# DeltaNet and max-out layer in one kernel: the order of the opening, and the first chunk's links by halves of the heads

## The chip, the cores and the metric

The kernel runs on one NeuronCore of a Trainium2 chip. A NeuronCore has a matrix engine (TensorE, in the profile PE, its weight loads PEld), a vector engine (VectorE, DVE), a scalar engine (ScalarE, ACT), a general engine (GpSimd, POOL) and a synchronising engine (SyncE, SP). Each runs its own list of instructions in order; DMA transfers are issued by SP, ACT or POOL. The metric is the device time of one execution in microseconds (us), as a median over executions.

## The reference

For 4 batches and 8 heads, 768 tokens with head size 48, the first half is a delta rule; its output, tokens by 384, goes through a layer of three products whose maximum is taken, and an output product:

```
k_n = k / (norm(k) + 1e-06)
for t in range(S):
    y[:, :, t] = einsum('bhd,bhde->bhe', q[:, :, t], state)
    v_old = einsum('bhde,bhd->bhe', state, k_n[:, :, t])
    state += beta_t * einsum('bhd,bhe->bhde', k_n[:, :, t], v_t - v_old)
x = y.transpose(0, 2, 1, 3).reshape(B * S, H * D)
out = max(x @ w1, x @ w2, x @ w3) @ w_out
```

The queries read the state before the step's own update. The four weights come in a 64-bit format (384 x 768 and 768 x 384).

## The kernel before

**Tiles.** The 768 tokens are cut into 12 chunks of 64. A unit n is two batches of one chunk (24 units); chunk c holds units 2c and 2c+1, and its 128 partitions are 64 tokens by 2 batches. Four units, that is two chunks, make a group m. Within a chunk the recurrence is solved as a triangular system: `turn` (L327) transposes keys and queries on PE and copies them to `kqt`, `gram` (L391) multiplies keys with keys (`at`) and keys with queries (`pt`, multiplied by a triangular mask at L412). `at` is written to DRAM and read back by `blocks` (L450) as 32 x 32 blocks, one block to a partition; `solve` (L470) takes the norms from the diagonal (L245 on ACT, then DVE) and runs a substitution on DVE, pairs of L508 and L512. For the first two groups it solves blocks of 16 (`FINE`), 15 pairs. The solved blocks go to DRAM (L517) and come back as `ut` (L526).

**Links.** For each of the first four chunks a chain of links follows, every one a set of small matmuls and an eviction from PSUM: `halves_z` (p_e, L574; it also transposes `ut` to `t` on DVE, L579), `halves_u` (p_f, L595; evictions with a minus sign at L603 and L605; then `turn_t1`, L558), `join_z` (p_z, L616), `join_u` (p_j, L629; evictions L631, L632), `old_k` and `old_q` (products with the state, none for chunk 0), `new` (p_u, L675), `step` (the state, p_s, L698), `to_y` (p_y, L715) and `to_x` (p_x, L732), whose copy `xt` is what the feed-forward part reads. `copied` (L777) splits an eviction of chunk 0 between ACT and DVE.

**Weights.** A weight is 24 pieces. `fetch` (L188) loads one into `w_bits` (5 buffers); `weights` (L198) converts it: an Abs (L211) and a product (L220) on ACT, a clamp (L215) on POOL, and for the piece before it two steps on DVE (L230, L234) and a sum on POOL (L238). Every step of the generator does the first half for one piece and the second half for the piece before.

**Order.** From the start to `by_hand.close()` (L936) every engine's list is in the order of the program text. Then, in the first feed-forward group (L993 to L1023), only PE's list is written by hand: `ffn(0)` gives 31 steps, the first 18 of 256 tokens each (matmuls p_h, L797; a maximum on DVE, L807), and after each step one conversion, one fetch, and the links that `FIRST` and `EARLY_LINKS` name for that step are written; three steps of the second group's solve belong to each of the first seven. There the framework's planner orders the lists of the other engines. The first nine steps read the tokens of chunk 0, the next nine those of chunk 1. Later groups are again all by hand.

**Opening.** Key loads of units 0 to 5 are issued on SP and ACT, half each (L151); units 6 and 7 later on ACT alone (L875). `busy` (L850) issues matmuls whose result nobody reads: six at the start, three after the first solve (L896), and one of 256 columns after each of six links (`between`, L905). The first squares and norms (L868, L876) scale the values of chunks 0 and 1 (L277).

## Time and profile before

| | |
|---|---|
| median of 4 executions | 601.01 us (599.02 to 601.82) |
| the profiled execution, its own time | 599.02 us |
| its span in the profile | 597.2 us |
| busy PE, DVE, ACT, POOL | 551.2, 350.5, 141.0, 120.3 us |
| first matmul of the feed-forward part (p_h) | 69.14 us |
| the tenth group of p_h, the first for chunk 1 | 113.91 us |
| PE busy from 150 to 300 us | 150.00 us |
| PE busy from 0 to 70 us | 45.40 us |
| DVE busy from 70 to 150 us | 69.23 us |

The profile gives for each instruction its engine, its line in the kernel, what it writes and reads, its start and length, and what its engine waited for before it. A row of the timeline reads: start, length, engine, line, operation, written tile <- read tile, shapes, count, and in brackets the idle time before it with what ended it. ACTq and SPq are the DMA issues of ACT and SP. A row of the table of windows gives the busy time of each engine in a stretch of the span, then the clock that TensorE was granted as a share of full, the DMA's share and its rate.

### The profile page before, as it was taken

Reading aid. Unit: us, or ns where it says so; the run is one execution under the profiler, and the core shown is the slowest. Engines: PE = TensorE matmul, PEld = TensorE weight load, DVE = VectorE, ACT = ScalarE, POOL = GpSimd, SP = SyncE. Lnnn points to the kernel's source line nnn. Section 1 sums busy time; section 2 is a strip of 40 time slices with the busy share of each in tenths; the row PEclk is TensorE's granted clock in tenths of the full one; section 3 lists DMA queues with packets and bytes.
Section 4 is the critical chain, followed back from the end, with each engine's and each line's share of the span. In section 5 each row is a group of like instructions: output and inputs, shape, how many; then the busy total and the mean of one; then the engine's idle time right before and its main releaser. Section 6 shows DMA issues by size and latency. Waiting matters only on the chain.

```text
span 597.2 us, 18730 instructions
## 1 busy us (share of the span) xinstructions
PE 551.2 (92%) x8120; PEld 324.6 (54%) x8120; DVE 350.5 (59%) x792; ACT 141.0 (24%) x281; POOL 120.3 (20%) x209
## 2 busy tenths in 40 slices
PE   6358969868999999999999999999999999999997
PEld 5235757756655555545555555545555455554444
DVE  2466699769359675499873699763898522211110
ACT  3224455644311122121112111221211111010000
POOL 6014544491010062000633002800001000000000
PEclk9555766998999999999999999999999999999999
DMA  8999874862430272454565283743743202210002
GB/s 132 161 231 179 190 165 126 206 126 54 90 46 8 75 161 62 85 116 113 143 143 120 64 133 93 187 113 57 121 93 80 46 1 56 60 47 0 0 0 54
DMA packets 159506, 58.78 MB, mean 98 GB/s; under 512 B 141184, under 2 KB 153280, under 8 KB 159424
## 3 DMA queue, kind: packets, MB, share of 16 engines
q1 hardware_dynamic: 141664, 43.52, 36.4%
q10 hardware_dynamic: 14560, 9.24, 6.2%
q0 software_dynamic: 3200, 4.82, 3.3%
q8 instruction: 64, 1.05, 0.8%
q14 instruction: 18, 0.15, 0.1%
HBM read 40.21 MB, written 17.30 MB: 96 GB/s over the span
## 4 chain that ended last, share of the span: by engine, by line
PE 63%; DVE 5%; DMA 4%; SPq 4%; issue 1%; ACT 0%; POOL 0%; DVEq 0%; ACTq 0%; POOLq 0%
PE p_h L797 39%; PE p_o L821 13%; PE p_g L402 2%; PE p_u L675 2%; PE p_y L715 2%; PE p_s L698 1%; DMA kpad<-in_k_dram 1%; PE p_k L647 1%; PE p_q L647 1%; SPq L366 1%; PE p_j L629 1%; DMA y_x<-y 1%; SPq L115 1%; PE p_z L616 1%; DVE y_bl L512 1%
## 5 line engine op out<-in xcount | busy, mean ns | idle before, releaser
L797 PE MATMUL p_h<-xt,w_sb 128*128 128x512 f32 (+1 forms) x702 | 303.1, 577 | 1.2 <-DVE xt L783 1.2
L797 PEld LDWEIGHTS p_h<-xt,w_sb 128*128 128x128 f32 x702 | 130.1, 194 | 122.5 <-issue 112.1
L807 DVE TENSOR_TENSOR h<-h,p_h 128x512 f32<-128x512 f32 (+1 forms) x78 | 50.2, 643 | 105.2 <-PE p_h L797 105.0
L821 PE MATMUL p_o<-wo_sb,h 128*128 128x384 f32 x288 | 94.6, 487 | 0.0
L821 PEld LDWEIGHTS p_o<-wo_sb,h 128*128 128x128 f32 x288 | 54.2, 190 | 37.2 <-issue 1.0
L512 DVE TENSOR_TENSOR y_bl<-y_bl,tmp 128x31 f32<-128x31 f32 (+20 forms) x139 | 53.6, 386 | 4.7
L277 POOL TENSOR_TENSOR v_t<-v_t,nrm 128x768 f32<-128x768 f32 x12 | 18.0, 1497 | 189.5 <-DMA turned<-in_k_dram 83.1
L366 POOL DMA_DIRECT2D turned<-in_q_dram x96 | 52.3, 552 | 3.6 <-POOL turned L361 3.1
L508 DVE TENSOR_TENSOR tmp<-x_bl,y_bl 128x31 f32<-128x31 f32 (+20 forms) x139 | 45.9, 330 | 4.0
L805 ACT COPY h<-p_h 128x512 f32<-128x512 f32 (+1 forms) x39 | 21.5, 552 | 109.9 <-PE p_h L797 109.8
L402 PE MATMUL p_g<-kqt 48*64 48x64 f32 (+1 forms) x1280 | 33.2, 252 | 8.9 <-ACT kqt L342 6.5
L402 PEld LDWEIGHTS p_g<-kqt 48*64 48x64 f32 x1280 | 28.0, 151 | 17.5 <-ACT kqt L342 8.5
L829 ACT COPY o_sb<-p_o 128x384 f32<-128x384 f32 x24 | 11.4, 476 | 82.0 <-PE p_o L821 78.6
L215 POOL TENSOR_SCALAR mant<-mant 128x384 f32<-128x384 f32 x24 | 13.6, 568 | 50.3 <-ACT mant L211 50.2
L558 DVE STREAM_TRANSPOSE t<-ut 32x256 f32<-32x256 f32 x48 | 20.8, 433 | 4.8 <-DMA ut<-y_d 4.0
L238 POOL TENSOR_TENSOR w_sb<-mant,up 128x384 int32<-128x384 int32 x18 | 18.1, 1005 | 18.9 <-DVE mant L234 15.7
L420 ACT COPY at<-p_g 128x512 f32<-128x512 f32 x20 | 11.6, 584 | 42.0 <-DVE pt L412 39.5
L230 DVE TENSOR_SCALAR mant<-mant 128x384 uint32<-128x384 uint32 x24 | 13.8, 577 | 11.1 <-POOL mant L215 11.0
L412 DVE TENSOR_TENSOR pt<-p_g,mask 128x512 f32<-128x512 f32 x24 | 16.4, 686 | 6.5 <-PE p_g L402 6.3
L632 DVE TENSOR_SCALAR ut<-p_j 32x512 f32<-32x512 f32 x12 | 8.3, 689 | 20.2 <-ACT ut L631 20.1
L667 ACT COPY qs<-p_q 128x768 f32<-128x768 f32 x11 | 8.8, 798 | 46.4 <-DVE v_t L659 27.6
L675 PEld LDWEIGHTS p_u<-v_t,ut 64*64 64x64 f32 x768 | 13.6, 142 | 9.5 <-issue 6.7
(111 smaller groups left out, 514.7 us busy)
## 6 DMA issues: line engine op xcount, KB each, us to landing
at_d<-at SPq DMA_DIRECT2D x42, 128.0 KB
v_t<-in_v_dram SPq DMA_DIRECT2D x24, 192.0 KB
w_bits<-in_moe_w_dram ACTq DMA_DIRECT2D x12, 384.0 KB
turned<-in_q_dram POOLq DMA_DIRECT2D x96, 48.0 KB, 3.0
turned<-in_k_dram SPq DMA_DIRECT2D x96, 48.0 KB
out_dram<-o_sb SPq DMA_DIRECT2D x48, 96.0 KB
kpad<-in_k_dram SPq DMA_DIRECT2D x38, 96.0 KB
y_x<-y SPq DMA_DIRECT2D x16, 192.0 KB
```

The source lines that it names most:

```text
L238: nc.gpsimd.tensor_tensor(out=dst.bitcast(I32), in0=mant_v.bitcast(I32), in1=up_v, op=ALU.add)
L277: nc.gpsimd.tensor_tensor(out=vts[c], in0=vts[c], in1=nrm[:, :, :, None].to_broadcast([128, 2, H, D]), op=ALU.mult,)
L366: (nc.sync, nc.gpsimd)[i].dma_start(out=t[p0 : p0 + 32, bb, at : at + NP * 2 * D].rearrange("p (j x) -> p j x", j=NP), in_=(k, q)[i][2 * b ...
L402: nc.tensor.matmul(p_g[rows(bb ^ (g * i)), par, c0 : c0 + C * (1 + whole)], kq[:, 0], kq if whole else kq[:, i],)
L508: nc.vector.tensor_tensor(out=t_v, in0=row.to_broadcast(t_v.shape), in1=column.to_broadcast(t_v.shape), op=ALU.mult,)
L512: nc.vector.tensor_tensor(out=rest, in0=rest, in1=t_v, op=ALU.subtract)
L558: nc.vector.transpose(out=t1[c % NU][block(bb ^ g), g], in_=ut[c % NU][block(bb), g, :, 0:BL])
L675: nc.tensor.matmul(p_v[rows(bb ^ g), g, h], ut[c % NU][rows(bb), g, h], rhs[rows(bb), g, h],)
L797: nc.tensor.matmul(p_h, w_sb[i][:, t, f * 128 : (f + 1) * 128], xt[:, t, lo : lo + w], start=(t == 0), stop=(t == KT - 1),)
L805: nc.scalar.copy(h, p_h)
L807: nc.vector.tensor_tensor(out=h, in0=h, in1=p_h, op=ALU.max)
L821: nc.tensor.matmul(p_o, hs[f][:, i * 128 : (i + 1) * 128], wo_sb[:, f], start=(f == 0), stop=(f == FT - 1),)
```

## The change

The opening is written in another order, and the links take the heads of chunk 0 in two halves.

- Only units 0 to 3 are loaded on both queues; 4 and 5 follow on SP, 6 and 7 on SP after the first value load. The copy of unit 1's turned keys goes to DVE and that of its gram to ACT; its stores are split between SP and ACT.
- The first squares stand behind `blocks(0)`; `ksq` shares the buffers of `o_sb` instead of those of the conversions.
- The query grams of units 0 and 1 are evicted by a copy on ACT ahead of the substitution and masked in place on POOL, and `scale(0)` and the first conversion stand there too; so do the key grams of units 6 and 7, whose stores (`to_dram`) come after the solved blocks.
- Three fetches and two conversions follow the reads of `ut`; then one conversion behind each link (none between p_f and p_z), all fetches on SP. The opening begins nine conversions and finishes eight; before, eight and seven.
- `heads_of` gives for chunk 0 two halves of the heads, each in a PSUM tile of its own, evicted by ACT and DVE in turn, and for other chunks one whole set, evicted by ACT. `halves_t`, ahead of p_e, transposes `t` in three instructions instead of two, so that the second tile's rows are exchanged there and z is copied without an exchange. `halves_u` has two evictions on each engine for a set instead of four, `turn_t1` three transposes instead of four.
- The six `between` matmuls go, and of the three after the solve two remain.
- `halves_z(1)` is done in the opening, and `FIRST` names the later links of chunk 1 up to two steps earlier. The squares and norms of chunks 2 and 3 are written at steps 8 and 9 instead of both at 8.

The diff, cut:

```diff
-    for n in range(6):
+    for n in range(4):
         load_k(n, both_queues)
...
-            ksq = work.tile([128, H, D], FP32, name="ksq", tag="up", bufs=2)
+            ksq = work.tile([128, H, D], FP32, name="ksq", tag="o_sb")
...
-    def first_norms(ksum, kflip):
+    def flipped(kflip):
...
+        return p_n
+
+    def first_norms(ksum, p_n):
...
-        nc.scalar.copy(
+        copy(
...
+    def masked(t, of, engine=nc.vector):
+        engine.tensor_tensor(
+            out=by_par(t), in0=of,
+            in1=mask[:, None, None, :].to_broadcast([128, 2, NP, C]), op=ALU.mult,
+        )
+
-    def gram(n, parts=(0, 1), queues=one_queue, copy=nc.scalar.copy):
+    def gram(n, parts=(0, 1), queues=one_queue, copy=nc.scalar.copy, later=False):
...
-            nc.vector.tensor_tensor(
-                out=by_par(pt), in0=p_v[:, :, :, 1],
-                in1=mask[:, None, None, :].to_broadcast([128, 2, NP, C]),
-                op=ALU.mult,
-            )
+            if later:
+                copy(by_par(pt), p_v[:, :, :, 1])
+            else:
+                masked(pt, p_v[:, :, :, 1])
...
+        if queues:
+            to_dram(n, queues)
+
+    def to_dram(n, queues=one_queue):
+        m, cc, g, at = n // 4, n % 4 // 2, n % 2, ats[n]
...
     def turn_t1(c):
 
-        for bb, g in TILES:
+        t, u_t = t1[c % NU], ut[c % NU]
+        nc.vector.transpose(out=t[:, 0], in_=u_t[:, 0, :, 0:BL])
+        for bb in range(2):
             nc.vector.transpose(
-                out=t1[c % NU][block(bb ^ g), g], in_=ut[c % NU][block(bb), g, :, 0:BL]
+                out=t[block(1 - bb), 1], in_=u_t[block(bb), 1, :, 0:BL]
             )
 
     fine = {}
 
+    def halves_t(c):
+
+        fine[c] = [square("t") for g in range(2)]
+        src = [ut[c % NU][:, g].rearrange("p h x -> p (h x)") for g in range(2)]
+        dst = [t.rearrange("p h x -> p (h x)") for t in fine[c]]
+        nc.vector.transpose(out=dst[0], in_=src[0])
+        for bb in range(2):
+            nc.vector.transpose(out=dst[1][rows(1 - bb)], in_=src[1][rows(bb)])
+
+    def heads_of(c, name, w):
+        copies = (nc.scalar.copy,) if c else (nc.scalar.copy, nc.vector.tensor_copy)
+        n = H // len(copies)
+        for i, copy in enumerate(copies):
+            p_v = ps_two(name)[:, :, 0 : n * w]
+            yield (
+                range(i * n, i * n + n),
+                p_v.rearrange("p g (h x) -> p g h x", x=w), copy,
+            )
+
+    def span(hs):
+        return slice(hs[0], hs[-1] + 1)
+
     def halves_z(c):
+        if c not in fine:
+            halves_t(c)
         at = [ats[2 * c + g] for g in range(2)]
-        u_t = ut[c % NU]
-        second = u_t.rearrange("p g h (f two x) -> p g h f two x", two=2, x=HB)
-        p_e = ps_two("p_e")
...
-        fine[c] = [square("t") for g in range(2)]
-        for g in range(2):
-            nc.vector.transpose(
-                out=fine[c][g].rearrange("p h x -> p (h x)"),
-                in_=u_t[:, g].rearrange("p h x -> p (h x)"),
-            )
-        z = zs[c % NU]
-        nc.scalar.copy(z[:, 0], p_v[:, 0])
-        nc.scalar.copy(z[rows(0), 1], p_v[rows(1), 1])
-        nc.vector.tensor_copy(z[rows(1), 1], p_v[rows(0), 1])
+        second = ut[c % NU].rearrange("p g h (f two x) -> p g h f two x", two=2, x=HB)
+        for hs, p_v, copy in heads_of(c, "p_e", BL):
+            for i, h in enumerate(hs):
+                for bb, g in TILES:
+                    r = rows(bb)
+                    nc.tensor.matmul(
+                        p_v[rows(bb ^ g), g, i], at[g][r, h], second[r, g, h, :, 1]
+                    )
+            copy(zs[c % NU][:, :, span(hs)], p_v)
+
+    def negated(bb, to, of):
+        if bb:
+            nc.vector.tensor_scalar_mul(to, of, -1.0)
+        else:
+            nc.scalar.mul(to, of, -1.0)
 
     def halves_u(c):
         t, z = fine.pop(c), zs[c % NU]
...
-        for f in (0, 1):
-            for bb, g in TILES:
...
-                if bb:
-                    nc.vector.tensor_scalar_mul(to, of, -1.0)
-                else:
-                    nc.scalar.mul(to, of, -1.0)
+        for hs, p_v, _ in heads_of(c, "p_f", BL):
+            for i, h in enumerate(hs):
+                for bb, g in TILES:
+                    r = rows(bb ^ g)
+                    nc.tensor.matmul(p_v[rows(bb), g, i], t[g][r, h], z[r, g, h])
+            for f in (0, 1):
+                for bb in range(2):
+                    r = block(bb, f, HB)
+                    negated(
+                        bb,
+                        ut[c % NU][r, :, span(hs), BL * f + HB : BL * (f + 1)],
+                        p_v[r, :, :, HB * f : HB * (f + 1)],
+                    )
         turn_t1(c)
 
     def join_z(c):
...
-        nc.scalar.copy(z[block(0)], p_v[block(0)])
-        (nc.vector.tensor_copy if c else nc.scalar.copy)(z[block(1)], p_v[block(1)])
+        for hs, p_v, _ in heads_of(c, "p_z", BL):
+            for i, h in enumerate(hs):
+                for bb, g in TILES:
+                    r = block(bb, 1)
+                    nc.tensor.matmul(
+                        p_v[block(bb ^ g), g, i], at[g][r, h, 0:BL], second[r, g, h]
+                    )
+            nc.scalar.copy(z[block(0), :, span(hs)], p_v[block(0)])
+            nc.vector.tensor_copy(z[block(1), :, span(hs)], p_v[block(1)])
...
-        nc.scalar.mul(u12[block(0)], p_v[block(0)], -1.0)
-        nc.vector.tensor_scalar_mul(u12[block(1)], p_v[block(1)], -1.0)
+        for hs, p_v, _ in heads_of(c, "p_j", BL):
+            for i, h in enumerate(hs):
+                for bb, g in TILES:
+                    r = block(bb ^ g)
+                    nc.tensor.matmul(p_v[block(bb), g, i], t[r, g, h], z[r, g, h])
+            for bb in range(2):
+                negated(bb, u12[block(bb), :, span(hs)], p_v[block(bb)])
...
-        copied(c, u, p_v)
+        for hs, p_v, copy in heads_of(c, "p_u", D):
...
+            copy(u[:, :, span(hs)], p_v)
...
+                copy(y[:, :, span(hs)], p_v)
...
-    busy(6)
+    load_k(4)
+    load_k(5)
+    busy(6, ident)
     turn(0, (0,))
-    turn(1, (0,))
+    turn(1, (0,), nc.vector.tensor_copy)
     keys(0, one_queue, nc.vector.tensor_copy)
+    keys(1, both_queues)
     turn(2, (0,))
-    keys(1, one_queue, nc.vector.tensor_copy)
     turn(3, (0,))
     keys(2, both_queues, nc.vector.tensor_copy)
     keys(3, both_queues, nc.vector.tensor_copy)
     load_beta()
-    sums_0 = first_squares()
+    nc.gpsimd.memset(in_wo(1), 0.0)
     turn(4, (0,))
     turn(5, (0,))
     blocks(0, both_queues)
+    sums_0 = first_squares()
     load_q(0)
     load_q(1)
-    for n in (6, 7):
-        load_k(n, (nc.scalar, nc.scalar))
-    first_norms(*sums_0)
-    keys(4, one_queue, nc.scalar.copy)
-    keys(5, one_queue, nc.scalar.copy)
-    for n in range(2):
-        fetch(nc.sync)
+    first_norms(sums_0[0], flipped(sums_0[1]))
+    keys(4)
+    keys(5)
+    fetch(nc.sync)
     load_v(0)
+    fetch(nc.sync)
+    load_k(6)
+    load_k(7)
     some(solving, 1)
     for n in range(2):
         turn(n, (1,))
+        gram(n, (1,), None, later=True)
+    for n in range(2):
+        masked(pts[n], by_par(pts[n]), nc.gpsimd)
+    scale(0, nrm_0[:, 0])
+    some(conv, 1)
+    for n in (6, 7):
+        turn(n, (0,))
+        keys(n, None)
+    some(solving, HB)
+    busy(2, solved[0].rearrange("p j i -> p (j i)")[:, 0:TOK])
+    some(solving, 2)
+    for n in range(3):
+        fetch(nc.sync)
+    some(conv, 2)
+    to_dram(6)
+    to_dram(7)
+    halves_z(0)
+    fetch(nc.sync)
+    some(conv, 1)
+    blocks(1)
+    halves_u(0)
+    load_v(1)
+    fetch(nc.sync)
+    join_z(0)
+    some(conv, 1)
+    fetch(nc.sync)
+    join_u(0)
+    some(conv, 1)
+    fetch(nc.sync)
+    old_k(0)
+    old_q(0)
+    new(0)
     some(conv, 1)
     fetch(nc.sync)
     load_q(2)
-    for n in range(2):
-        fetch(nc.sync)
-    some(solving, HB)
-    for n in range(2):
-        gram(n, (1,))
-    for n in (6, 7):
-        turn(n, (0,))
-        keys(n, (nc.scalar, nc.scalar), nc.scalar.copy)
-    busy(3, TOK, solved[0].rearrange("p j i -> p (j i)")[:, 0:TOK])
+    to_y(0)
+    halves_z(1)
     some(conv, 1)
-    some(solving, 2)
-    blocks(1)
     fetch(nc.sync)
-    scale(0, nrm_0[:, 0])
-    some(conv, 2)
-    solving = solve(1)
-
-    def between():
-        busy(1, 256, kpad[0][:, 0:4].rearrange("p h d -> p (h d)"))
-
-    halves_z(0)
-    between()
-    load_v(1)
-    some(conv, 1)
-    fetch()
-    halves_u(0)
-    between()
-    join_z(0)
-    between()
-    join_u(0)
-    between()
-    fetch()
-    some(conv, 1)
-    old_k(0)
-    old_q(0)
-    new(0)
-    between()
-    fetch()
-    to_y(0)
-    between()
-    some(conv, 1)
-    fetch()
     to_x(0)
     load_q(3)
     load_q(4)
     load_v(2)
     some(conv, 1)
-    fetch()
+    fetch(nc.sync)
+    solving = solve(1)
     by_hand.close()
     tc.no_sync_barrier()
     scale(1, nrm_0[:, 1])
@@ -953,8 +976,8 @@
     }
 
     FIRST = {
-        0: "s0 e1 T2", 1: "k1 f1 P2 T3", 2: "z1 P3", 3: "q1 j1", 4: "u1 T4",
-        5: "y1 T5", 6: "s1 P4", 7: "x1 T6", 8: "P5 T7", 12: "P6", 14: "P7",
+        0: "f1 s0 T2", 1: "z1 k1 P2 T3", 2: "j1", 3: "P3 q1", 4: "u1 T4",
+        5: "y1", 6: "s1 T5 P4", 7: "x1 T6", 8: "P5 T7", 12: "P6", 14: "P7",
     }
 
 
@@ -1002,9 +1025,8 @@
             load_v(3)
         if 5 <= i < 9:
             load_k(3 + i)
-        if i == 8:
-            prep(2)
-            prep(3)
+        if i in (8, 9):
+            prep(i - 6)
         if i == 12:
             load_q(11)
         if i in (15, 18):
```

## The prediction

> **What bounds the kernel now.** I read the page's 40 slices first, then the table of windows, then the timelines of the opening. From 150 us on TensorE never stands (10.00 of 10, then 40.00 of 40), so the end follows from the point at which that stretch begins; the change touches what lies before it. There two things bind: until 69.14 us (the first feed-forward matmul) a chain of single steps, and after it VectorE.
>
> ```profile
> 80.00:90.00 10.00, 8.02 (x168) 6.43 (x163) 9.67 (x28) 4.91 (x13) 3.54 (x6) 0.50 0.57 156
> 90.00:100.00 10.00, 9.60 (x187) 7.25 (x184) 9.78 (x24) 4.56 (x9) 4.89 (x6) 0.56 0.41 127
> 100.00:110.00 10.00, 8.72 (x228) 7.40 (x219) 9.69 (x26) 6.75 (x13) 2.98 (x4) 1.00 0.58 113
> ...
> 150.00:160.00 10.00, 10.00 (x246) 6.57 (x245) 3.72 (x6) 3.94 (x6) 0.00 (x0) 1.00 0.43 85
> ```
>
> Columns: window, PE, PEld, DVE, ACT, POOL busy, granted clock, DMA share, GB/s. DVE is busy 97% from 80 to 110, so PE's 1.5 us groups come 3 to 11 us apart. The chain before 69 us, from the timelines of the queues and engines:
>
> ```profile
> 17.11 1.03 ACTq L460 DMA_DIRECT2D x_bl<-at_d  x2
> 18.17 5.96 ACTq L115 DMA_DIRECT2D kpad<-in_k_dram  x4
> 25.25 0.27 ACT L245 ACTIVATE root_bl<-x_bl 128x32 f32<-128x32 f32 x1
> ...
> 37.44 0.50 SPq L517 DMA_DIRECT2D y_d<-y_bl  x1
> 41.30 0.50 SPq L517 DMA_DIRECT2D y_d<-y_bl  x1
> 44.52 0.37 ACTq L526 DMA_DIRECT2D ut<-y_d  x1
> 47.13 1.94 PE L574 MATMUL p_e<-ut,at 64*64 64x32 f32 x64 [1.76 <-DMA ut<-y_d]
> ```
>
> ACT issues four key loads for 5.96 us while the first solve waits for its root on ACT. The solve ends at 37.37; its second store is held to 41.30, while the DMA moves 313 to 363 GB/s (weights issued at 33.74). Then the links run:
>
> ```profile
> 56.65 0.57 ACT L619 COPY z<-p_z 32x512 f32<-32x512 f32 x1 [1.85 <-PE p_z L616]
> 57.25 0.58 ACT L620 COPY z<-p_z 32x512 f32<-32x512 f32 x1
> 57.63 1.30 PEld L629 LDWEIGHTS p_j<-z,t 32*32 32x32 f32 x64 [0.65 <-ACT z L619]
> ```
>
> Each link is some 2 us of matmuls at a clock of 0.50 and then an eviction of 1.1 us in two copies, one after the other.
>
> **The change part by part** (times in the profiled execution: span 597.2, 599.02 with what lies around it; the median of the four runs is 601.01, 2.0 above).
>
> 1. Key loads 4 and 5 leave ACT's queue: two issues of 5.59/6 = 0.93, and kqt copies are split between ACT and DVE. The first copy moves from 7.84 to about 6.1, but SP now has eight load issues (to 8.65) before the first store. Walking the stores (0.8 each) the last issue ends at 13.7 instead of 14.86, so ACT's x_bl read moves from 17.11 to 16.0: −1.1.
> 2. Loads 6 and 7 (5.96) leave ACT; the squares come instead. First square to last reduce was 13.68 to 16.38 = 2.7; then p_n and root 0.6, the grams of 4 and 5 behind them on PE (1.99 for 64 matmul records at 0.50, as at 28.51), the last at copy 0.6: root_bl at 17.0 + 2.7 + 0.6 + 2.0 + 0.4 = 22.7 against 25.25: −2.55. x_bl's landing is not shown; from an issue end at 17.0 and the 2.25 that ut needs (44.89 to 47.13) it comes by 20, so it is covered. If it took until 25, this step is worth 0; without the grams ahead, −4.
> 3. The masks move off DVE (2 x 0.64 at 37.28, where DVE then idles to 44.3: worth nothing) to POOL, in place, and scale(0) (1.58, now at 45.20) comes forward: both fall into the substitution. Neither form of mask is in the trace; L277 gives 1.497/768 x 512 = 1.0, L238 1.005/384 x 512 = 1.34; I take 1.0, being the same operation. What POOL costs DVE:
>
> ```profile
> 32.06 0.50 POOL L215 TENSOR_SCALAR mant<-mant 128x384 f32<-128x384 f32 x1 [21.56 <-ACT mant L211]
> 32.17 0.54 DVE L512 TENSOR_TENSOR y_bl<-y_bl,tmp 128x126 f32<-128x126 f32 x1
> ...
> 132.23 2.03 DVE L248 TENSOR_TENSOR newton<-newton,ksum 128x16 f32<-128x16 f32 x1
> 132.74 1.49 POOL L277 TENSOR_TENSOR v_t<-v_t,nrm 128x768 f32<-128x768 f32 x1
> ```
>
> The first lost 0.25 (0.54 against 0.29) of POOL's 0.50, the second ends when POOL does (0.16 undisturbed). So each POOL instruction costs its length less about 0.2: 1.0 + 1.0 + 1.5 + 0.5 − 0.75 = 3.25; bounds 2.0 (half, as in the first pair) and 4.7 (all, masks at 1.34). Solve end: 37.37 − 2.55 − 0.25 + 3.25 = 37.8.
>
> The Trainium skill, "SBUF — State Buffer", section "Who interferes with whom", speaks against this part: a VectorE instruction with two SBUF inputs and a GpSimd one that reads SBUF exclude each other for the whole instruction. The second pair agrees, the first only half; by the rule (4.0 in place of 3.25) the sum below would be 0.75 less gain.
>
> 4. Round trip through DRAM. Three fetches now stand behind the ut reads and two stand ahead of loads 6 and 7, issued by about 30, so no weights are in flight at 37.8 and I take the hold of 3.4 to go: stores 0.6, landing 41.30 to 44.51 = 3.2, ut 44.52 to 47.13 = 2.6: p_e at 37.8 + 6.4 = 44.2 instead of 47.13. If the hold stays: 47.6.
> 5. What is late next: the third conversion. Its ScalarE operation stands ahead of the first z copy on ACT and needs the third fetch, which SP issues after all six ut reads (five from 44.51 to 47.0 = 2.5), thus at 37.8 + 6.3. A fetch took 27.37 to 31.42 = 4.0 to its first use, so 48.1; with 0.55 + 0.53 for the conversion and 0.36 for the copy p_f starts at 49.6 (now 50.15): −0.55. What SP carries behind it: two more fetches, stores of 6 and 7 (2.6), x_bl of chunk pair 1 (from about S + 13, S the solve's end, landing by S + 18; needed after the first group, now at 72.5), values, fetches, queries 3 and 4 by about S + 27 = 65; now SP is through at 64, so nothing is late. Bounds: no wait, 46.3 (transposes of t: three of 0.65 from 44.2, they are not slowed beside POOL at 49.26); a landing 3 later, 52.6.
> 6. Links, counted from p_f (0). Halves of p_f to 1.4 and 2.8; four evictions of 0.27 to 0.29 each half, still in turn as at 53.01 to 55.44, end at 2.9 and 4.1; turn_t1 (now three of 0.43) 5.4; p_z meanwhile; z copies on DVE behind it 5.8 and 6.2; p_j to 7.3; a conversion's DVE part to 7.4; u12 7.85 and 8.25; p_u to 10.2; u copies 9.6 and 10.8; p_y to 12.5; p_e of chunk 1 to 14.5 (2.0, moved here); p_x 16.0; xt behind a conversion's 1.1 on ACT 17.3. Now it is 69.14 − 50.15 = 19.0: −1.7, though p_e(1) is done inside. Bounds: every eviction hidden and no conversion in the way, 14; DVE the bound (10.5 us of links and six conversions of 0.91 + 1.5 POOL time), 25. I take 17.3, nearer to the row, as ACT and PE have room. First feed-forward matmul: 49.6 + 17.3 = 66.9: −2.2 in all.
>
> The six dummies between the links (1.22 each, beside the evictions) and one of three before them go; the granted clock was 0.50 from 50 to 65 although PE was busy 14.4 of 15 us with them, so I charge nothing. "TensorE: Matmul & The Clock Gate", Part 1, would have about 3.4 us of activity lift the clock; by that the links, warm with the dummies, would lose up to half of 14.4 = 7 us without them, an estimate from that page; the row differs.
>
> 7. From first (69.14) to tenth matmul group (113.91) is 44.8 us, DVE-bound. Leaving it: two transposes of t for chunk 1 (1.40) and a z copy (0.42), one conversion (0.35 + 0.56, and 0.6 of waiting for POOL: L230's mean of 545 ns against 355, and other stretched rows, make some 11 us over 18), four evictions made two (0.3), a turn_t1 transpose (0.43): −4.1. Bounds: −6 with more locks gone, 0 if chains rather than DVE bind.
> 8. Chunks 2 and 3: transposes +0.7 each, z copy −0.42, evictions −0.3, t1 −0.43: −0.9, of which I take −0.5 as DVE is half idle from 110 to 130; bounds −2 and +2. The squares no longer share the conversions' buffers (L267 waited 1.8 for POOL): on ACT, 24% busy, so nothing. The POOL memsets put elsewhere end by 11.5, ahead of their readers. From 150 on nothing on PE is added; turn_t1's fewer instructions lie beside PE.
>
> Sum: −2.2 − 4.1 − 0.5 = −6.8: 592.2 for the profiled execution, 601.01 − 6.8 = 594.2 for the median.
>
> **Rivals.** (a) **The opening gives nothing**: masks and scale cost 4.7, the third fetch lands 1 to 2 later; first group at 69, only parts 7 and 8 remain: 597. For it: ACT and SP wait in order, and eight conversions share DVE with the links. Chance 0.16. (b) **No wait for the third fetch and little lock**: p_f at 45 to 46, 594.2 − 4.5 = 590. For it: step 4's quiet DMA; against: SP's order. Chance 0.10. (c) **It cancels**: opening 3 to 5 later (links DVE-bound, 25), parts 7 and 8 give it back: 601. Chance 0.11. (d) **Slower: PE stands in its hand-written order between groups 1 and 10.** f1, z1 and j1 of chunk 1 move one or two groups forward, while DVE and ACT keep a planner's order. From p_f's end to its last eviction was 7.0 us (80.9 to 87.9), p_z's 4.0, p_j's 3.5, 14.5 in all, now covered by groups that come earlier. It decides when DVE runs dry for more than 6.8 + 1.8 us of these; all 14.5 would give 594.2 + 14.5 = 609, and 606 is its middle. Against: DVE was idle only 0.9 of 30 us. Chance 0.21.
>
> **How the numbers follow.** Forecast 0.42 (591 to 597.5), (a) 0.16, (b) 0.10, (c) 0.11, (d) 0.21. 0.3% is 1.8 us, about what a measurement of this kernel can tell from no change. Faster: 0.42 + 0.16 + 0.10 = 0.68; within: 0.11; slower: 0.21. The range from 588 to 603 leaves out most of (d) and a little of (b).
>
> **What would show it.** root_bl at 22.7; POOL masks beside stretched L508/L512 rows; the two y_d stores 0.5 apart; ACT idle for w_bits ahead of the first z copy; p_e(1) before the first p_h; DVE still near 97% after it, but ten groups in 40.7 us. Wrong if x_bl lands late, if the stores are still held apart, or if DVE idles between groups 1 and 10.

## The result, and the profile after

The changed kernel takes 597.45 us (median of 53 executions, 593.21 to 603.46), the kernel before 600.7 on the same chips (79 executions): a ratio of 0.9941, 95% interval 0.9928 to 0.9954. By the ratio that is 3.5 us less, by the medians 3.25, where 6.8 were forecast. Ratios, here and below, leave out executions that the chip ran in its slower state, so they are not quite those of the medians. The profiled execution took 596.05 us, its span 594.1, against 599.02 and 597.2.

I cut the span at six points that both traces have: the root that starts the first substitution (L245), the end of the solve, the first matmul of p_e, of p_f, the first and the nineteenth group of feed-forward matmuls p_h (the first eighteen take 256 tokens each, those of chunk 0 or of chunk 1; the nineteenth is the first that takes the 512 of both), and the end.

| stretch | before | after | change | forecast |
|---|---|---|---|---|
| start to root | 25.25 | 22.70 | −2.55 | −2.55 |
| root to end of solve | 12.12 | 15.07 | +2.95 | +3.0 |
| solve to p_e | 9.76 | 6.58 | −3.18 | −3.4 |
| p_e to p_f | 3.02 | 4.86 | +1.84 | +2.4 |
| p_f to first p_h (links) | 18.99 | 19.15 | +0.16 | −1.7 |
| first to nineteenth p_h | 84.32 | 80.40 | −3.92 | −4.6 |
| nineteenth p_h to the end | 443.74 | 445.34 | +1.60 | 0 |
| span | 597.2 | 594.1 | −3.1 | −6.8 |

The timeline of the opening of the kernel after, as far as the root, the masks, the solve's stores and p_e (columns as before: start, length, engine, line, operation, written <- read, and in brackets the idle time before it with its releaser):

```profile
22.70 0.26 ACT L245 ACTIVATE root_bl<-x_bl 128x32 f32<-128x32 f32 x1
...
27.80 1.29 POOL L395 TENSOR_TENSOR pt<-pt,mask 128x512 f32<-128x512 f32 x1 [17.30 <-ACT pt L422]
28.00 1.22 DVE L519 TENSOR_TENSOR tmp<-x_bl,y_bl 128x110 f32<-128x110 f32 x1
...
31.90 1.52 POOL L277 TENSOR_TENSOR v_t<-v_t,nrm 128x768 f32<-128x768 f32 x1
32.12 1.45 DVE L523 TENSOR_TENSOR y_bl<-y_bl,tmp 128x128 f32<-128x128 f32 x1
...
35.06 0.27 DVE L519 TENSOR_TENSOR tmp<-x_bl,y_bl 128x110 f32<-128x110 f32 x1
37.84 1.14 SPq L528 DMA_DIRECT2D y_d<-y_bl  x2
...
44.35 1.31 PE L611 MATMUL p_e<-ut,at 64*64 64x32 f32 x64 [1.34 <-DMA ut<-y_d]
```

The root comes when it was forecast. The two stores of the solve are issued together (before, the second followed 3.9 after the first). Each POOL instruction stretches the VectorE instruction that meets it until about its own end: the row of 1.22 is 0.27 when POOL rests. Then the waits of ACT, and of PE behind it:

```profile
47.92 0.54 ACT L211 ACTIVATE mant<-w_bits 128x384 f32<-128x384 f32 x1 [4.93 <-DMA w_bits<-in_moe_w_dram]
48.80 0.36 ACT L614 COPY z<-p_e 128x256 f32<-128x256 f32 x1
49.21 1.93 PE L628 MATMUL p_f<-z,t 64*64 64x32 f32 x64 [3.55 <-ACT z L614]
49.31 6.29 SPq L471 DMA_DIRECT2D wo_sb<-at_d  x4
55.63 2.26 SPq L131 DMA_DIRECT2D v_t<-in_v_dram  x2
57.99 2.74 SPq L192 DMA_DIRECT2D w_bits<-in_moe_w_dram  x4
...
64.13 0.55 ACT L211 ACTIVATE mant<-w_bits 128x384 f32<-128x384 f32 x1 [4.24 <-DMA w_bits<-in_moe_w_dram]
65.02 0.46 ACT L748 COPY y<-p_y 128x384 f32<-128x384 f32 x1
```

The first wait (4.93) was forecast. The second was not: SP sits 6.29 us on four issues (the diagonal blocks of the second group, in a buffer named wo_sb; by the waits of SP's queue, 2.0 of it for the at_d stores just issued) and 2.26 on two value loads before it gets to the next four weights at 57.99; ACT reaches the seventh conversion (the expectation of e11 counts it as the sixth) and stands 4.24 us in front of it, and the eviction y of the link to_y, queued behind, comes that much later. PE stands 3.09 us before p_x, more than the 1.7 that the links were to gain. The 4.24 is that of one execution: e6 below, the same up to here, waits 2.18 us at this place, and e12, with dummies added, 1.92.

From 69 us on, the table of windows of the kernel after (window, PE, PEld, DVE, ACT, POOL busy, granted clock, DMA share, GB/s):

```profile
80.00:90.00 10.00, 7.04 (x169) 6.29 (x170) 9.71 (x23) 4.94 (x11) 3.42 (x5) 0.50 1.16 188
90.00:100.00 10.00, 8.64 (x248) 6.78 (x247) 9.38 (x24) 5.80 (x12) 6.12 (x8) 1.00 0.54 141
100.00:110.00 10.00, 7.58 (x185) 6.22 (x186) 9.76 (x27) 6.40 (x15) 5.00 (x5) 1.00 0.85 223
...
150.00:160.00 10.00, 10.00 (x211) 5.26 (x209) 2.07 (x3) 3.04 (x5) 0.00 (x0) 1.00 0.42 93
```

VectorE is as full as before (28.85 of 30 us against 29.14), and from 150 on PE hardly stands (1.0 of the 150 us to 300; before, not at all). The third group of p_h, though, comes at 88.02, later than before (84.14); the tenth comes at 113.29 (113.91), and only by the nineteenth are 4.7 us won (148.76 against 153.46). Ahead of the third group ACT waits for weights a third time, and PE stands three times:

```profile
77.76 0.55 ACT L211 ACTIVATE mant<-w_bits 128x384 f32<-128x384 f32 x1 [2.91 <-DMA w_bits<-in_moe_w_dram]
...
78.60 0.42 DVE L618 TENSOR_SCALAR ut<-p_f 16x256 f32<-16x256 f32 x1 [0.26 <-ACT ut L620]
...
80.19 0.32 PE L646 MATMUL p_z<-ut,at 32*32 32x32 f32 x4 [4.27 <-ACT kqt L345]
81.78 1.06 PE L646 MATMUL p_z<-ut,at 32*32 32x32 f32 x60 [1.27 <-DVE ut L618]
...
86.37 0.69 DVE L650 COPY z<-p_z 32x512 f32<-32x512 f32 x1
...
87.12 1.11 PE L339 MATMUL p_t<-ident,qpad 128*128 128x128 f32 x4 [1.50 <-DVE z L650]
```

The wait for weights costs little here: VectorE has its own list to do until 78.3 and stands only 0.26 us for the eviction that came late on ACT. Two kernels of the next section that don't wait for a weight at this place, e3 and e4, have their third group as long after the first (19.5 and 20.2 us; here 19.7, before 15.0). PE stands at p_z of chunk 1, which its new order puts ahead of the group: first for ACT, which has the evictions of p_f and a kqt copy to do, then for VectorE's eviction, and once more behind it for the copy of z. That order is a part of the delay only: with p_z back behind the group (e6) it is still 17.7 us.

### The profile page after: what moved, and what is told of

Its sections match the earlier page's. It is cut to its first block, busy times and chain, and to the rows that moved or that the text cites. A ratio compares the mean times of both kernels' runs of the same rounds, so it can differ in the third digit from the quotient of the medians.

```text
span 594.1 us, 18707 instructions
## 1 busy us (share of the span) xinstructions
PE 540.5 (91%) x8106; PEld 319.4 (54%) x8106; DVE 348.0 (59%) x776; ACT 140.2 (24%) x274; POOL 122.1 (21%) x211
## 3 DMA queue, kind: packets, MB, share of 16 engines
q8 instruction: 63, 1.03, 0.7%
## 4 chain that ended last, share of the span: by engine, by line
PE 60%; DVE 18%; DMA 10%; SPq 4%; issue 3%; POOL 2%; ACT 2%; ACTq 0%; DVEq 0%; POOLq 0%
PE p_h L823 37%; PE p_o L847 11%; DVE tmp L519 4%; DVE y_bl L523 3%; PE p_g L411 3%; DMA kpad<-in_k_dram 2%; DMA y_d<-y_bl 2%; PE p_u L704 1%; PE p_y L744 1%; DMA ut<-y_d 1%; PE p_k L676 1%; PE p_s L726 1%; DMA at_d<-at 1%; PE p_j L659 1%; DMA w_bits<-in_moe_w_dram 1%
## 5 line engine op out<-in xcount | busy, mean ns | idle before, releaser
L519 DVE TENSOR_TENSOR tmp<-x_bl,y_bl 128x31 f32<-128x31 f32 (+20 forms) x139 | 48.0, 345 | 4.0
L395 DVE TENSOR_TENSOR pt<-p_g,mask 128x512 f32<-128x512 f32 x22 | 15.2, 689 | 8.9 <-PE p_g L411 8.7
L211 ACT ACTIVATE mant<-w_bits 128x384 f32<-128x384 f32 x24 | 13.4, 556 | 28.3 <-DMA w_bits<-in_moe_w_dram 12.1
L646 PE MATMUL p_z<-ut,at 32*32 32x32 f32 x768 | 11.5, 204 | 9.1 <-ACT kqt L345 4.3
L618 DVE TENSOR_SCALAR ut<-p_j 32x512 f32<-32x512 f32 (+1 forms) x13 | 8.3, 647 | 18.6 <-ACT ut L620 18.5
L646 PEld LDWEIGHTS p_z<-ut,at 32*32 32x32 f32 x768 | 9.4, 115 | 17.2 <-ACT kqt L345 4.7
```

Of the source, the lines that this page charges most:

```text
L395: engine.tensor_tensor(out=by_par(t), in0=of, in1=mask[:, None, None, :].to_broadcast([128, 2, NP, C]), op=ALU.mult,)
L519: nc.vector.tensor_tensor(out=t_v, in0=row.to_broadcast(t_v.shape), in1=column.to_broadcast(t_v.shape), op=ALU.mult,)
L646: nc.tensor.matmul(p_v[block(bb ^ g), g, i], at[g][r, h, 0:BL], second[r, g, h])
```

## The experiments

My theory after the result: the opening and the links lose to **conversions waiting for weights**, in order on ACT, because SP issues the fetches late. Rivals: the masks on POOL inside the substitution are the larger loss; halves are worth nothing anyway; PE's hand-written order holds PE at chunk 1's links; the missing dummies cost clock. Diffs are against the changed kernel unless said. Ratios are to the kernel before on the same chip, with 95% intervals (6 to 12 executions each, 0.25 to 0.45% either way); the stretches are those of the table above.

| run | median us | ratio [95%] | root to solve | solve to p_e | p_e to p_f | links | 1st to 19th p_h |
|---|---|---|---|---|---|---|---|
| after | 597.45 | 0.9941 [0.9928, 0.9954] | 15.07 | 6.58 | 4.86 | 19.15 | 80.40 |
| e1 masks late | 596.97 | 0.9886 [0.9841, 0.9931] | 13.25 | 7.57 | 5.89 | 17.16 | 82.21 |
| e2 fetch, ahead of keys | 595.44 | 0.9890 [0.9853, 0.9927] | 15.08 | 9.71 | 1.47 | 17.29 | 82.19 |
| e3 e1 and e2 | 596.70 | 0.9916 [0.9888, 0.9943] | 13.26 | 10.60 | 1.38 | 18.52 | 80.77 |
| e11 fetch, behind keys | 595.78 | 0.9908 [0.9878, 0.9938] | 15.09 | 6.53 | 1.41 | 18.97 | 86.46 |
| e5 masks, fetch behind keys | 591.63 | 0.9829 [0.9784, 0.9874] | 12.12 | 8.77 | 1.27 | 17.57 | 81.73 |
| e9 e5, places as in e6 | 590.71 | 0.9810 [0.9770, 0.9851] | 12.11 | 8.43 | 1.58 | 17.58 | 81.54 |
| e10 e5, whole links | 592.34 | 0.9861 [0.9830, 0.9893] | 12.11 | 8.64 | 1.63 | 20.00 | 81.85 |
| e4 whole links | 599.96 | 0.9961 [0.9931, 0.9990] | 15.08 | 6.71 | 5.33 | 19.07 | 82.29 |
| e7 before, with halves | 602.67 | 1.0004 [0.9979, 1.0030] | 12.19 | 9.65 | 2.76 | 19.14 | 85.04 |
| e6 places of before | 594.48 | 0.9875 [0.9846, 0.9904] | 15.07 | 6.62 | 5.53 | 17.15 | 79.62 |
| e8 p_e(1) back as well | 600.08 | 0.9967 [0.9942, 0.9992] | 15.07 | 6.50 | 6.79 | 16.62 | 85.69 |
| e12 dummies back | 597.03 | 0.9943 [0.9913, 0.9973] | 15.09 | 6.38 | 5.12 | 17.42 | 81.44 |

The root is left out: with the opening up to it the same, the changed kernel and all runs but e7 have it between 21.63 and 24.08, so an absolute time early in a single profile is good to a microsecond or so.

**e1: the masks on VectorE behind the solve**

```
-    for n in range(2):
-        masked(pts[n], by_par(pts[n]), nc.gpsimd)
-    scale(0, nrm_0[:, 0])
     some(conv, 1)
...
     some(solving, HB)
     busy(2, ...)
+    for n in range(2):
+        masked(pts[n], by_par(pts[n]))
+    scale(0, nrm_0[:, 0])
     some(solving, 2)
```

> The changed kernel with the two query masks on DVE (in place in SBUF) and scale(0) behind the first substitution instead of on POOL inside it. Theory 'lock' (each POOL instruction inside the substitution costs DVE its length less about 0.2): the four stretched DVE rows go except the one beside L215, the first solve ends at 34.6 to 35.0 instead of 37.8, p_e starts at 41.2 to 41.6 instead of 44.35, and if the opening's gain reaches the end the time is 2 to 3 us under the changed kernel (about 594.5 to 595.5, ratio to the kernel before near 0.990). Rival 'absorbed' (the stretch between the first and the nineteenth p_h group is set by DVE and the planner's order whatever the opening does): solve as early, but the time stays within 1 us of the changed kernel, ratio 0.993 to 0.995.

Root to solve falls by 1.82, for two masks of 1.29: 0.91 each. The scale still runs on POOL inside the substitution, since POOL has nothing queued ahead of it. What the solve wins is lost in the two stretches behind it: ACT now waits 6.01 for the third weight, and p_e to p_f grows by 1.03. Alone, the masks' place brings nothing to the profile as far as p_f (26.71 from the root against 26.51); the ratio is 0.55% better, with intervals that just overlap.

**e2: the three fetches ahead of the key loads of units 6 and 7; e3: e1 and e2 together**

```
     load_v(0)
-    fetch(nc.sync)
+    for n in range(4):
+        fetch(nc.sync)
     load_k(6)
...
-    for n in range(3):
-        fetch(nc.sync)
     some(conv, 2)
```

> The changed kernel with the three fetches that follow the reads of ut issued ahead of key loads 6 and 7. Theory 'ACT stands in order for the third fetch' (4.9 us idle ahead of L211 at 47.92): that wait goes, the first z copy follows p_e at once, p_f starts at about 47.1 (set by the three transposes of t) instead of 49.21, first p_h 1 to 2 earlier, time 0 to 2 under the changed kernel. Rival 'the hold comes back': with weights in flight when the solve ends, the second y_d store is held up to 3.4 us as in the kernel before, p_e starts up to 3.4 later and the time is 1 to 3 us over the changed kernel.

> Both edits: masks and scale(0) behind the substitution, and the three fetches ahead of key loads 6 and 7. 'lock' and 'ACT in order' together: p_f at 44 to 45 instead of 49.21, first p_h 3 to 5 earlier than 68.36 unless the later fetch wait (4.2 us of ACT at 64.13) grows by as much; time 2 to 5 under the changed kernel. 'absorbed': within 1 us of it. 'The hold comes back': the solve then ends nearer to the fetches, p_e no earlier than 44, time as the changed kernel or up to 2 over.

The fetch wait is gone (p_e to p_f 1.47), and the round trip takes 3.1 more: the key loads, now behind four weights, come late, and with them the grams of units 6 and 7 on PE, with the dummies behind them, after which p_e starts without a break; and on ACT a copy that stands ahead of its ut reads. The trace of e2:

```profile
38.26 1.09 PE L339 MATMUL p_t<-ident,kpad 128*128 128x128 f32 x4 [8.07 <-DMA kpad<-in_k_dram]
...
44.25 0.85 ACTq L537 DMA_DIRECT2D ut<-y_d  x2
```

A wait was moved, not removed. It is the same mechanism as in the changed kernel, at another load. Still, e2's ratio is 0.5% below that of the changed kernel, its interval just clear of it (0.9927 against 0.9928), though the nineteenth group comes no earlier in the profile (148.71 against 148.76): a gain that the profile doesn't explain. e3, which was to be 2 to 5 us faster, has p_e as late (10.60 behind the solve), and its time isn't told apart from that of the changed kernel. So the next two runs put the fetches behind the keys.

**e11: the fetches behind the key loads; e5: that, and the masks and the scale late**

```
     load_k(6)
     load_k(7)
+    for n in range(3):
+        fetch(nc.sync)
     some(solving, 1)
...
     some(solving, 2)
-    for n in range(3):
-        fetch(nc.sync)
     some(conv, 2)
```

e5 also takes the masks to VectorE as e1 does, and writes the scale behind `some(conv, 2)`.

> The changed kernel with only the three fetches moved ahead of the substitution, behind the key loads of units 6 and 7; masks and scale stay on POOL. If the waits for the third and the sixth fetch are what the opening lost, both go: p_f at 46 instead of 49.21, first feed-forward matmul at 64.5 to 65.5 instead of 68.36, 3 us less in all, ratio about 0.989; with the run that also moves the masks at 0.983 the masks are then worth the other 0.6%. Rival: the fetches share the DMA with the solve's stores and the second store is held again by some 3 us, p_e at 47.5, nothing gained, ratio 0.994.

> The changed kernel with the masks on DVE behind the first substitution, scale(0) behind the two conversions that follow it (so that POOL is kept out of the substitution but for one L215), and the three fetches behind key load 7, ahead of y_d. Solve 12.1 to 12.4 us after root_bl instead of 15.07. Theory 'opening passes through': p_f at 44 to 46, first p_h 3 to 5 earlier than 68.36, nineteenth p_h 3 to 5 earlier than 148.76, time 3 to 5 under the changed kernel (ratio to the kernel before 0.986 to 0.989). Rival 'absorbed by the planner's stretch': first p_h as early, nineteenth p_h within 1.5 of 148.76, ratio 0.992 to 0.995. Rival 'hold': the second y_d store is held up to 3.4 by the weights in flight, p_e no earlier than 44.

In e11 the first p_h comes at 64.70, 3.66 earlier, and the y_d stores are not held (solve to p_e 6.53), so that rival is out. What had held the second store in the kernel before was, by the waits of SP's queue there (engine, line, what it waited for: us in total, times, longest), not a weight but a store of a gram:

```profile
SPq L517 <- DMA at_d<-at: 3.4, 1, 3.4
```

The new opening has the stores of units 6 and 7 behind the solved blocks. But the third group of e11 comes at 89.01, because the next weight is missing there. The trace of e11:

```profile
70.04 0.61 SPq L192 DMA_DIRECT2D w_bits<-in_moe_w_dram  x1
...
78.75 0.54 ACT L211 ACTIVATE mant<-w_bits 128x384 f32<-128x384 f32 x1 [7.35 <-DMA w_bits<-in_moe_w_dram]
...
79.58 0.42 DVE L618 TENSOR_SCALAR ut<-p_f 16x256 f32<-16x256 f32 x1 [4.76 <-ACT ut L620]
...
81.17 0.31 PE L646 MATMUL p_z<-ut,at 32*32 32x32 f32 x4 [9.40 <-ACT kqt L345]
```

A fetch issued at 70.04 is waited for until 78.75, at a DMA share of 1.08 between 70 and 80; behind the conversion on ACT stand an eviction of p_f, for which VectorE waits 4.76 us (0.26 in the changed kernel), and a kqt copy, and behind that PE for 9.40 us. The gain of the opening was given back here in this execution: the nineteenth group comes at 151.16, 2.4 later than after. The median is nevertheless not above that of the changed kernel (intervals overlap): undecided between a small gain and none.

In e5 the opening is shorter by the masks, too, and the corresponding wait is 3.36 instead of 7.35. Its substitution is as short as before (12.12), though solve to p_e takes 2.2 more than in the changed kernel: p_e starts there without a break behind the dummies, which on PE stand behind the grams of units 6 and 7; and with the fetches on their way the stores can be read back later, too (4.69 us from their issue to the first ut read, 3.07 in the changed kernel). From root to first p_h it needs 39.73 us, the kernel before 43.89, the changed kernel 45.66. Its lead over the changed kernel is 1.1%, with intervals that lie apart. In the profiles e1 and e11 alone each ended in another wait for weights. That it needed both moves isn't shown by the times: the leads of e1 (0.55%) and e11 (0.33%) add up to nearly as much.

**e4, e7, e10: what the halves are worth**

```
-        copies = (nc.scalar.copy,) if c else (nc.scalar.copy, nc.vector.tensor_copy)
+        def by_tile(to, of):
+            nc.scalar.copy(to[:, 0], of[:, 0])
+            nc.vector.tensor_copy(to[:, 1], of[:, 1])
+
+        copies = (nc.scalar.copy if c else by_tile,)
```

e10 is this edit in e5. e7 goes the other way: the kernel before, with its own opening, dummies and places, and the new link functions with halves for chunk 0.

> The changed kernel without the halves: heads_of gives chunk 0 one set of all heads too, with ACT and DVE each evicting one tile (the other evictions as in the halves, on twice the width). Theory 'halves overlap': the links from p_f to the first p_h last 2 to 4 us longer than 19.15, p_f starts some 0.5 later, and the time is 2 to 4 over the changed kernel, about the kernel before. Rival 'the links are set by fetches and conversions on ACT': first p_h within 1 us of 68.36 and the time within 1 us of the changed kernel.

> The kernel before with the links by halves alone (heads_of, halves_t, turn_t1 in three, the new evictions); opening, fetches, masks, dummies, FIRST as before. Theory 'halves overlap': from p_f to the first p_h 16 to 17 us instead of 19.0, first p_h at 66 to 67.5, time 1.5 to 3 under the kernel before (ratio 0.995 to 0.9975). Rival 'nothing without the new order': ratio 0.998 to 1.002, the dummies and one eviction after another fill the place of the overlap.

> Masks on DVE behind the solve, three early fetches, and the links of chunk 0 whole again (one PSUM tile, the eviction split by units between ACT and DVE). If the halves were worth nothing in the changed kernel because the waits for weights stood over them, they now show: links from p_f to the first feed-forward matmul 19 to 20 instead of 17.6, 1.5 to 2.5 us slower in all, ratio 0.986 to 0.987. Rival: halves change nothing, because an eviction of half the size is not half as long: links 17.6, ratio 0.983.

In the changed kernel and in the kernel before, the links differ by under 0.2 us with halves or without (19.07 against 19.15; 19.14 against 18.99). But neither pair of profiles is clean. At the seventh conversion the changed kernel waits 4.24 and e4 only 0.34; e6 and e12, which have the halves and wait 2.18 and 1.92 there, have links of 17.15 and 17.42. And in e7 PE stands 2.72 us in the links for nothing that the profile shows; without that they would be 16.4, as forecast:

```profile
61.11 0.86 PE L659 MATMUL p_j<-z,t 32*32 32x32 f32 x47 [2.72 <-issue]
```

In e5, where no wait of more than 2 us stands over them, whole links take 20.00 and halves 17.57: 2.4 us. So by the profiles halves are worth some 2 us of the links, and a later wait can absorb that. The times settle none of it: the intervals of e4 and the changed kernel overlap, so do those of e10 and e5, and e7 takes as long as the kernel before.

**e6 and e8: the places of chunk 1's links**

```
-        0: "f1 s0 T2", 1: "z1 k1 P2 T3", 2: "j1", 3: "P3 q1", 4: "u1 T4",
-        5: "y1", 6: "s1 T5 P4", 7: "x1 T6", 8: "P5 T7", 12: "P6", 14: "P7",
+        0: "f1 s0 T2", 1: "k1 P2 T3", 2: "z1 P3", 3: "q1 j1", 4: "u1 T4",
+        5: "y1 T5", 6: "s1 P4", 7: "x1 T6", 8: "P5 T7", 12: "P6", 14: "P7",
```

e8 takes `halves_z(1)` out of the opening as well, and FIRST as it was before: `0: "s0 e1 T2", 1: "k1 f1 P2 T3"`, and the rest as in e6.

> The changed kernel with p_f of chunk 1 still behind group 1, but z1, P3, j1 and T5 at the steps the kernel before has (z1 behind group 3 instead of group 2). Theory 'PE stands in its hand-written order' (rival d of the prediction): group 3 comes at 77 to 82 instead of 88.02, since it no longer stands behind z1's wait for the evictions of p_f; if that order costs at the end, the nineteenth group is 1.5 to 4 earlier and the time 1.5 to 4 under the changed kernel. Rival 'only moved': group 3 is earlier, the tenth and nineteenth groups and the time stay within 1 us, or become later by up to 3 as chunk 1's chain starts later.

> The changed kernel with p_e of chunk 1 taken out of the opening and FIRST as in the kernel before (e1 behind group 1, f1 behind group 2). First p_h up to 2 earlier than 68.36 (p_e of 1.9, transposes and a copy gone from ahead of it). Theory 'DVE work moved out of the stretch is gain' (step 7 of the prediction): the stretch from the first to the nineteenth group is 1.5 to 3 longer than 80.4, time 0 to 2 over the changed kernel. Rival 'it is neutral': time within 1 us.

These two ran on the same chip and differ in the place of p_e(1), and with it of p_f(1), which in e8 comes one group later. With p_e(1) in the opening the links cost 0.53 more (17.15 against 16.62), and the first eighteen groups 6.1 less (79.62 against 85.69): the medians differ by 5.6 us, with intervals apart. The 6.1 are the upper end: the three profiles without p_e(1) in the opening (before, e7, e8) have 84.3 to 85.7 in that stretch, those with it 79.6 to 82.3, e11 apart. It is the one part of the change whose gain shows by itself, though e8, which has all the rest, is still at 0.9967. Of the 6.1 us, 4.9 come between the tenth and the nineteenth group (38.15 against 33.28), behind the windows in which VectorE is full; so that it is VectorE's time which is saved isn't shown. e6 against the changed kernel is less plain. Its median is 0.7% better, intervals apart, but the profiles differ by only 0.8 us between first and nineteenth group, and the 2.0 in the links comes from instructions that the edit doesn't touch (the second fetch wait, 2.18 instead of 4.24, came out shorter). In e6 PE also stands, before p_k instead of p_z, and the third group came at 85.55, later than I had expected:

```profile
81.88 1.96 PE L676 MATMUL p_k<-st,kqt 48*64 48x48 f32 x64 [6.33 <-DVE st L732]
...
85.55 1.89 PE L823 MATMUL p_h<-xt,w_sb 128*128 128x256 f32 x6
```

**e12: the six dummies back, one behind each link of chunk 0**

```
+    def between():
+        busy(1, kpad[0][:, 0:4].rearrange("p h d -> p (h d)"))
     halves_z(0)
+    between()
...
```

> The changed kernel with the six matmuls of 256 columns that nobody reads put back, one behind each link of chunk 0. The prediction charged nothing for taking them out. If the granted clock does not depend on them here: clock 0.50 as before, and a loss of 0 to 3 us, since PE has less idle time to hide 1.22 each. Rival, from the skill's page on the clock: the clock rises during the links and they take some 3 to 7 us less, ratio 0.983 to 0.989.

The time is unchanged (0.9943 against 0.9941), but the reason given for that in the forecast, a clock that doesn't answer, is wrong. The kernel after first, then e12 (windows, columns as above):

```profile
50.00:55.00 5.00, 3.24 (x111) 2.55 (x107) 3.75 (x11) 3.48 (x10) 1.74 (x4) 0.50 0.85 220
55.00:60.00 5.00, 4.67 (x170) 4.24 (x174) 4.19 (x10) 3.32 (x8) 2.70 (x4) 0.50 0.81 144
60.00:65.00 5.00, 2.44 (x94) 2.30 (x88) 2.88 (x5) 0.87 (x2) 0.24 (x1) 0.50 0.96 309
```

```profile
50.00:55.00 5.00, 4.99 (x140) 3.28 (x135) 3.88 (x11) 2.91 (x10) 1.67 (x3) 0.50 0.97 193
55.00:60.00 5.00, 5.00 (x104) 3.59 (x100) 3.45 (x8) 3.12 (x7) 2.46 (x3) 0.50 1.00 252
60.00:65.00 5.00, 3.51 (x116) 2.82 (x112) 3.57 (x7) 3.23 (x7) 2.28 (x4) 0.96 1.05 262
```

With the dummies PE is busy without a break from 48.2, and at 60 to 61 the clock rises to 1.00; p_e(1) takes 1.14 instead of 1.90, p_x 0.95 instead of 1.55. That is late, and only two links profit; the links are 1.7 shorter in this profile, which the shorter second fetch wait (1.92 against 4.24) alone would give.

**e9: e5 with the places of e6**

> Masks on DVE behind the solve, three fetches behind the key loads of units 6 and 7, and FIRST in the kernel before's places for chunk 1 (only p_f one step earlier). If the places of chunk 1's links in PE's hand-written order hold PE (the third group at 85.55 instead of 88.02 when only they were put back), the two gains add: third group at about 79 instead of 81.31, first group of the second 256 tokens 1.4 us earlier, ratio 0.979 to 0.982, time about 590. Rival: with the opening seven us shorter, DVE alone binds behind it and the order of PE's list matters no more: same as the run without it (0.983), or 1 us slower.

0.981 against 0.983: the same within the intervals, and the same in the profile from root to nineteenth group (121.24 against 121.46). The places no longer matter here, so e6's lead stays unexplained. e9 is the fastest kernel of the study, 590.71 us: 1.9% below before, and with an interval that lies wholly below that of the changed kernel.

## Why the prediction was right or wrong

The sign was right, the size half. The median, 597.45, lies at the very edge of the forecast (591 to 597.5), nearer to rival (a)'s 597 than to 594.2. In the profiled executions 3.7 us of the gain are missing: 1.85 in the links, 0.7 between the first and the nineteenth group, 1.6 behind it, with 0.4 more than forecast won elsewhere. By its own steps:

1. **Steps 1 and 2, root at 22.7: right** (22.70; the other runs with this opening have 21.63 to 24.08, so that it agrees so closely is luck).
2. **Step 3, POOL's price: right in sum** (+2.95 for +3.0), with a wrong part: a mask takes 1.29, not 1.0, and costs 0.91 (e1), so 0.38 of it is hidden where I took about 0.2. The Trainium skill's rule ("SBUF — State Buffer", section "Who interferes with whom": the two engines exclude each other for the whole instruction) agrees with the rows in kind: the VectorE row that meets a mask ends 0.13 after it. What it costs is less than the whole length, as the waiting instruction's own time lies inside. The masks' old place behind the solve, which I had as "worth nothing" to leave, is the better one for the substitution: with the masks there it takes 13.25 (e1), with the scale behind it as well 12.12 (e5).
3. **Step 4, the hold goes: right in size** (−3.18 for −3.4), **not in its reason.** I had put the hold down to the weights in flight. In e11, with three fetches issued from 31.36, and in e5, with the solve ended at 33.85 just behind them, the two stores are issued within 1.14 us all the same. SP's queue in the kernel before names a store of a gram, and the new opening has those of units 6 and 7 behind the solved blocks. So the term came true, as far as these rows show, by an edit that I had not charged with it.
4. **Step 5, the wait for the third fetch: right** (p_f 49.21 for 49.6). Its next sentence failed: "SP is through at 64, so nothing is late". SP began its last query loads at 64.59, about as forecast, but I had asked only whether those come in time, not the fetches between: behind 6.29 us of x_bl issues they landed too late, and the seventh conversion waited 4.24.
5. **Step 6, links in 17.3: failed by 1.85**, for this reason and not for the link itself. With the same links and waits of 1.3 to 2.2 at that conversion e1, e2, e5, e6, e9 and e12 measured 17.15 to 17.58 (e3, with 1.27, is the exception: 18.52). In e6 everything up to there is the changed kernel's own, so part of the 1.85 belongs to the one execution. I had walked the chain of links with conversions as work on ACT, and not as something that may itself have to wait.
6. **The dummies at nothing: the price was right, the argument not** (e12). The row it rested on, 0.50 while PE was busy 14.4 of 15 us, holds, but doesn't say that the clock can't answer: in the kernel before it rose at 68, after PE had run without a break from 54.55. The Trainium skill's 3.4 us ("TensorE: Matmul & The Clock Gate", Part 1) would have had it rise by 52 in e12; it rose at 60 to 61. Where the matmuls are large the runs are nearer to the rule: after the first dummy of 512 columns the clock was up within 2.3 us in the changed kernel (at 42.2, PE busy without a break since 38.83), 3.4 in the kernel before and up to 5.0 in the others.
7. **Steps 7 and 8, −4.6 between first and nineteenth group: −3.92, right in sum, not in place.** From the first to the tenth group nothing was won (44.93 against 44.77, where I had named 40.7 as a sign); the gain came from there to the nineteenth (35.47 against 39.55), where I had taken 0.5. Step 7 counted VectorE's work and left out that PE, in its new order, would stand behind chunk 1's links: 7.0 us between the second and the third group, before 4.6. And its parts were mis-sized: moving p_e(1) gives up to 6.1 (e6 against e8), for which my working had 1.8 of VectorE's time (1.40 + 0.42); the rest of step 7, without that move, gives nothing that shows (e8's stretch is 85.69, before's 84.32). Why the move gives more than its busy time is not settled.
8. **"From 150 on nothing": +1.60** behind the nineteenth group, but not in waits. The same 5634 matmuls keep PE busy 438.35 us there against 436.80, and PE stands 6.99 against 6.94. This stretch took between 443.9 and 447.7 in the profiles of the experiments (443.94 in e1, 447.69 in e2, whose edits end long before it; 446.49 in e7, which has the order of the kernel before); the kernel before, with 443.74, lies below them all. A cost of the change can't be told from what differs between executions.

Of the rivals, (a) has the time (597) and half its grounds: ACT and SP do wait in order, and the first group comes only 0.8 us earlier. But the masks and the scale cost 2.95, not 4.7, the third fetch is not later than forecast, and what took the links' gain in the profile is the fetch for the seventh conversion. (d)'s mechanism is there in small: PE stands 4.27 us before chunk 1's p_z, z waits on VectorE till 86.37, and the third group comes 3.9 later than before. By the tenth group the two kernels are level, and whether it costs anything in the end stays open (e6 says 0.7%, e9 nothing).

## What to carry to other kernels

Follow a prefetch as far as the in-order engine that consumes it: an operation that waits for a weight holds every eviction queued behind it, so a new place for a fetch is worked out against the issue times of everything ahead of it on its queue, under load. Then ask what the next engine would have done meanwhile: behind a wait of 2.91 us on ACT VectorE stood 0.26, behind one of 7.35 it stood 4.76. A gain in a chain can be taken by a later wait in the same stretch; in the profiles the halves and the moved masks showed theirs when the fetches had been moved as well. A whole link moved out of a crowded stretch can pay more than its busy time (p_e of chunk 1: 1.8 us on VectorE, 2 to 6 us of the stretch).

## What the runs showed of the hardware

- A DMA issue is not a fixed price: four reads of x_bl kept SP for 6.29 us in the changed kernel, 4.3 of it without a wait for data (1.1 each), while the same four took 2.56 in the kernel before.
- A fetch of one size was waited for until 4.0 us after its issue in the opening of the kernel before (DMA share 0.89), and until 8.7 us in e11 (1.08).
- In the links, whose matmuls are 64 x 64 or 32 x 32 with one dummy of 256 columns between, the granted clock rose only after 12 and 13.5 us of unbroken PE work in e12 and the kernel before, but after 6.2 in e7 (from 61.11), and stayed at 0.50 where there were gaps (the changed kernel, 7.91 of 10 us busy between 50 and 60). After the first of the dummies of 128 x 128 by 512 it rose in 2.3 to 5.0 us in all fourteen profiles. So PE's busy time in a profile doesn't tell when the clock rises; that the size of the matmuls is the reason was not tried.
- A POOL product of two SBUF operands with a broadcast one, 128 x 512, takes 1.29 us and costs a VectorE chain 0.91.
- In the kernel before the second store of the solve stood 3.4 us on SP's queue for an earlier store of a gram; in e5 and e11, where weights were on their way, the two stores were issued within 1.14 us.
